# Chunk bounds from fp16 halves, q rings filled by transfers, and a new order, in a chunk-selecting attention with a feed-forward layer

## The chip, the cores and the metric

The kernel runs on one core of a Trainium2 chip. The core has five engines that run side by side, each through its own list of instructions in order: TensorE (matmuls; PE in the profile, with its weight loads as PEld), VectorE (DVE), ScalarE (ACT), GpSimd (POOL) and SyncE (SP, which here only issues transfers). The metric is the device time of one execution in microseconds, the median of the runs.

## The reference

Attention over 4 batches, 8 heads, 768 positions and head width 64, in which each query sees only six chunks of 32 keys, followed by a normalised feed-forward layer. Cut to what matters:

```python
k_min = np.min(k_chunks, axis=3)                  # per chunk of 32 keys
k_max = np.max(k_chunks, axis=3)
ub = np.sum(np.maximum(q * k_min, q * k_max), -1) # upper bound of a query with a chunk
ub = np.where(causal, ub, -1e9)
top_chunks = np.argsort(ub, axis=-1)[..., -6:]
scores = scale * q @ k.T
scores = np.where(chosen chunk and pos_q >= pos_k, scores, -1e9)
attn = softmax(scores) @ v
# x = attn with the heads side by side: (4, 768, 512)
xn = (x - mean) / sqrt(var + 1e-6) * g_ln
out = x + relu(xn @ w_ch1) @ w_ch2                # hidden width 2048
```

The bounds decide which chunks are chosen, so they need nearly fp32 accuracy: two chunks whose bounds are close must not change places.

## The kernel before

Two heads are handled together as a pair: head 0 on partitions 0 to 63, head 1 on 64 to 127. There are 16 pairs, four for each batch; pairs 0 to 3 (batch 0) take another path through loads and turning than pairs 4 to 15 (`HP` is 4). For pairs 4 to 15, q and k come in by 128-byte rows so that a VectorE transpose of 32x32 blocks turns them (`turn`); the parts that matter:

```python
prp = ctx.enter_context(tc.tile_pool(name="prp", bufs=2))
...
def turn(g, nm, i=None):
    if g >= HP:
        t = prp.tile([P, S], F32, name=nm + "T", tag=nm + "T")
        nc.vector.transpose(t, st[g][nm].rearrange("p c e -> p (c e)"))
        ...
def qpos(g, i=None):                     # relu of q; pairs 4 to 15 on VectorE
    ...
            else:
                nc.vector.tensor_scalar_max(st[g][nm][:, u:], qt[:, u:], 0.0)
                st[g]["q32"] = qt
def qring(g, i=None):                    # q as fp16 into the rings, times 128
    nc.scalar.activation(QA[g % NK][0:64, ...], qt[0:64, :], ACTF.Copy, scale=QS)
    nc.scalar.activation(QB[g % NK][64:P, ...], qt[64:P, :], ACTF.Copy, scale=QS)
def kbound(g, i=None):                   # chunk minima and maxima of k
    nc.vector.tensor_reduce(kc[:, 0, n], view, axis=AX.X, op=ALU.min)
    nc.vector.tensor_reduce(kc[:, 1, n], view, axis=AX.X, op=ALU.max)
def kdiag(g, i=None):                    # one block for each head, on GpSimd for g >= HP
    ...
        eng.tensor_tensor(kc[:, 1], kc[:, 1], kc[:, 0], ALU.subtract)
    eng.tensor_tensor(bd, kc..., hsel..., ALU.mult)
def bounds(g, i=None, idle=0):
    ...
    nc.tensor.matmul(ub, ident_b, causb[...], start=True, stop=False)   # causal -1e30
    for s in range(a, z):                # 5 query tiles
        for nm, arr in (("q32", 0), ("r32", 1)):
            nc.tensor.matmul(ub[:, s - a]..., st[g][nm][:, ...],        # fp32, 48 columns
                             st[g]["bd"][:, arr], start=False, stop=...)
def select(g, i=None):                   # threshold by the 8 greatest; then the mask
    for s in range(z - a):
        for hh in range(2):
            nc.vector.max(m8[:, s, hh, :], ub[:, s, hh, :])
    nc.vector.tensor_tensor(mn..., ub, m8[..., 6:7]..., ALU.is_le)
```

The bound is written as q times k_min plus relu(q) times (k_max minus k_min), so that two products give it. After `select`, `maskt` turns the mask on TensorE and `mring` copies it beside q into the ring; `smm` forms scores from the rings, `sexp` the exponentials on ScalarE, `diag` the causal edge on GpSimd, `values` the product with v, `norm` the division. `pstat`, `centre`, `xt`, `xcopy`, `m1`, `relu`, `m2`, `rstd` and `fin` are the feed-forward layer of each half batch. All steps stand in one string, `ORDER`, and on every engine the instructions run in its order; the engines wait for each other by data alone. `idle` and `warm` are matmuls without a use of their result[...].

Of the kernel before, what the change touches and what calls it, by code (L numbers as in the profile page):

```python
# [19 lines left out]
def kernel(  # L20
# [30 lines left out]
    QS = 128.0  # L51
    HS = 64.0
# [6 lines left out]
    vap = ctx.enter_context(tc.tile_pool(name="vap", bufs=6))  # L59
# [15 lines left out]
    causb = const.tile([P, NT - 1, 2, NCH], BF16, name="causb", tag="causb")  # L75
    RT = const.tile([P, S], F16, name="RT", tag="RT")
# [9 lines left out]
    BD = [ring.tile([P, 2, 2, NCH], F32, name=f"BD{i}", tag=f"BD{i}") for i in range(NB)]  # L86
    NM = 3
# [14 lines left out]
    def consts():  # L102
# [18 lines left out]
        nc.vector.memset(hsel[0:64, 0, 1:2], -1.0)  # L121
        nc.vector.memset(hsel[64:P, 0, 0:1], -1.0)
        nc.vector.memset(hsel[0:64, 1:3, 1:2], 1.0)
        nc.vector.memset(hsel[64:P, 1:3, 0:1], 1.0)
# [6 lines left out]
    def late():  # L131
        nc.gpsimd.memset(mhalf, -0.5)

# [67 lines left out]
    def turn(g, nm, i=None):  # L201
        if g >= HP:
            t = prp.tile([P, S], F32, name=nm + "T", tag=nm + "T")
            nc.vector.transpose(t, st[g][nm].rearrange("p c e -> p (c e)"))
            st[g][nm, i] = t
            return
        pst = ps_t.tile([P, 512], F32, name="tr", tag="one")
        src = st[g][nm, i]
        for t in range(TR):
            nc.tensor.transpose(pst[:, t * P:(t + 1) * P], src[:, t], ident_f)  # L210
        st[g][nm, i] = pst[:, 0:TR * P]

    def qpos(g, i=None):
        qt = st[g]["qn", i]
        a, z = span(g, i)
        u = P if a == 0 else 0
        signs = (("q32", -1.0), ("r32", 1.0)) if g < HP else (("r32", 1.0),)
        for nm, sign in signs:
            st[g][nm] = prp.tile([P, qt.shape[1]], F32, name=nm, tag=nm)
            if g < HP:  # L220
                nc.scalar.activation(st[g][nm][:, u:], qt[:, u:], ACTF.Relu, scale=sign)
            else:
                nc.vector.tensor_scalar_max(st[g][nm][:, u:], qt[:, u:], 0.0)
                st[g]["q32"] = qt

    def qring(g, i=None):
        qt = st[g]["qn", i]
        a, z = span(g, i)
        nc.scalar.activation(QA[g % NK][0:64, a * P:z * P], qt[0:64, :], ACTF.Copy, scale=QS)  # L229
        nc.scalar.activation(QB[g % NK][64:P, a * P:z * P], qt[64:P, :], ACTF.Copy, scale=QS)  # L230

# [20 lines left out]
    def kdiag(g, i=None):  # L252
# [10 lines left out]
        )  # L263

    def bounds(g, i=None, idle=0):
        a, z, n = chosen(g, i)
        full = ps_t.tile([P, 512], F32, name="ub", tag="one")
# [15 lines left out]
    def select(g, i=None):  # L283
# [3 lines left out]
        m8 = smp.tile([P, NT - 1, 2, 8], F32, name="m8", tag="m8")  # L287
        for s in range(z - a):
            for hh in range(2):
                nc.vector.max(m8[:, s, hh, :], ub[:, s, hh, :])  # L290
# [193 lines left out]
    def fin(b, r, i, e=None):  # L484
# [13 lines left out]
        rinit.0 ld.0.0 ld.1.0 rinit.2 rinit.3 ldv.0.0 ld.2.0 rinit.1 consts warm.8 ld.3.0 ldv.0.1 turn.0.kn.0  # L498
        turn.0.qn.0 kbound.0.0 kdiag.0.0 rrows.1.1 ld.0.1 ldv.2.0 qpos.0.0 kcopy.0.0 turn.1.kn.0 rrows.0.0 kcopy.1.0
        qring.0.0 bounds.0.0.6 turn.1.qn.0 turn.2.kn.0 qpos.1.0 kbound.1.0 select.0.0 maskt.0.0 kdiag.1.0 qring.1.0  # L500
        rrows.3.0 ldv.1.0 kbound.2.0 mring.0.0 bounds.1.0.6 turn.2.qn.0 rrows.1.0 kcopy.2.0 smm.0.0.0 qpos.2.0
        rrows.2.0 ldv.3.0 turn.3.kn.0 kdiag.2.0 select.1.0 bounds.2.0.6 maskt.1.0 kbound.3.0 mring.1.0 qring.2.0
        sexp.0.0.0 select.2.0 smm.0.0.1 kcopy.3.0 turn.3.qn.0 sexp.0.0.1 qpos.3.0 diag.0.0 smm.1.0.0 turn.0.kn.1
        maskt.2.0 qring.3.0 kdiag.3.0 sexp.1.0.0 w1.1.3 bounds.3.0.6 values.0.0 kbound.0.1 mring.2.0 smm.1.0.1
        kcopy.0.1 select.3.0 diag.1.0 smm.2.0.0 w1.0.2 norm.0.0 maskt.3.0 sexp.1.0.1 mring.3.0 values.1.0 smm.2.0.1
        norm.1.0 sexp.2.0.0 sexp.2.0.1 pstat.0.0 smm.3.0.0 diag.2.0 sexp.3.0.0 values.2.0 smm.3.0.1 pstat.1.0
        diag.3.0 sexp.3.0.1 norm.2.0 values.3.0 pstat.2.0 norm.3.0 w1.2.3 w1.3.3 pstat.3.0 ld.1.1 turn.0.qn.1
        kdiag.0.1 qpos.0.1 qring.0.1 turn.1.qn.1 centre.0.0 turn.1.kn.1 idle.5 qpos.1.1 ld.3.1 kcopy.1.1 ld.2.1
        ldv.1.1 kbound.1.1 w2.2.1 idle.4 w2.0.0 w2.1.0 qring.1.1 xt.0.0.3 ldb.4.kn xt.0.0.0 xt.0.0.2 xcopy.0.0.0
        xt.0.0.1 xcopy.0.0.2 xcopy.0.0.3 rrows.3.1 xcopy.0.0.1 bounds.0.1 ldb.4.qn rrows.0.1 turn.2.kn.1 select.0.1  # L510
        m1.0.0.0 kcopy.2.1 relu.0.0.0 turn.2.qn.1 qring.2.1 late maskt.0.1 kbound.2.1 mring.0.1 kdiag.1.1 rstd.0.0
        kdiag.2.1 m1.0.0.2 relu.0.0.2 qpos.2.1 m1.0.0.6 relu.0.0.6 m1.0.0.8 m1.0.0.4 turn.4.kn relu.0.0.8 relu.0.0.4
        m1.0.0.10 smm.0.1.0 bounds.1.1 turn.3.kn.1 relu.0.0.10 select.1.1 smm.0.1.1 sexp.0.1.0 sexp.0.1.1
        turn.3.qn.1 ldb.5.kn qpos.3.1 m1.0.0.12 kbound.4 kbound.3.1 relu.0.0.12 maskt.1.1 m1.0.0.14 smm.0.1.2
        bounds.2.1 kdiag.3.1 turn.4.qn kcopy.3.1 mring.1.1 w2.3.1 relu.0.0.14 smm.0.1.3 qpos.4 sexp.0.1.2 kdiag.4
        bounds.3.1 ldb.5.qn qring.3.1 smm.1.1.0 rrows.2.1 select.2.1 sexp.0.1.3 bounds.4 diag.0.1 sexp.1.1.0
        smm.1.1.3 sexp.1.1.3 select.3.1 smm.1.1.2 sexp.1.1.2 maskt.2.1 select.4 maskt.3.1 values.0.1 mring.2.1
        smm.1.1.1 m2.0.0.0.0 diag.1.1 kcopy.4 smm.2.1.0 m2.0.0.1.0 mring.3.1 sexp.1.1.1 smm.2.1.2 ldv.2.1 values.1.1
        sexp.2.1.0 sexp.2.1.2 norm.0.1 turn.5.kn smm.2.1.1 ldv.3.1 maskt.4 kbound.5 smm.3.1.0 pstat.0.1 m2.0.0.1.1
        sexp.2.1.1 norm.1.1 mring.4 m2.0.0.0.1 sexp.3.1.0 smm.2.1.3 turn.5.qn kdiag.5 qring.4 diag.3.1 smm.3.1.2  # L520
        sexp.2.1.3 m2.0.0.1.2 m2.0.0.0.2 sexp.3.1.2 smm.3.1.3 sexp.3.1.3 ldb.6.kn smm.4.1.0 diag.2.1 pstat.1.1
        m2.0.0.0.3 qring.5 fin.0.0.0 ldb.7.kn ldb.6.qn ldv.4 m2.0.0.1.3 smm.3.1.1 ldb.7.qn ldb.8.kn sexp.3.1.1
        ldb.8.qn ldv.6 fin.0.0.1 values.2.1 m2.0.0.2.0 sexp.4.1.0 ldv.5 values.3.1 qpos.5 smm.4.0.0 norm.2.1 kcopy.5
        m2.0.0.2.1 pstat.2.1 smm.4.1.3 sexp.4.0.0 norm.3.1 m2.0.0.2.2 diag.4.0 sexp.4.1.3 smm.4.1.1 m2.0.0.2.3
        smm.4.1.2 pstat.3.1 centre.0.1 sexp.4.1.1 sexp.4.1.2 fin.0.0.2 xt.0.1.1 smm.4.0.1 xt.0.1.3 xt.0.1.0 xt.0.1.2
        ldv.9 ldb.9.kn xcopy.0.1.0 xcopy.0.1.1 xcopy.0.1.2 bounds.5 xcopy.0.1.3 sexp.4.0.1 diag.4.1 turn.6.kn
        m1.0.1.0 kcopy.6 ldb.9.qn m1.0.1.2 relu.0.1.0 select.5 maskt.5 m1.0.1.4 relu.0.1.2 relu.0.1.4 m1.0.1.8
        turn.7.kn m1.0.1.6 relu.0.1.8 m1.0.1.14 relu.0.1.6 kbound.6 kdiag.6 ldv.7 values.4.0 mring.5 turn.6.qn
        kbound.7 qpos.6 kdiag.7 relu.0.1.14 smm.5.0.0 values.4.1 sexp.5.0.0 smm.5.0.1 rstd.0.1 bounds.6 norm.4.0
        pstat.4.0 turn.7.qn sexp.5.0.1 diag.5.0 qring.6 smm.5.1.0 values.5.0 qpos.7 smm.5.1.1 sexp.5.1.0 norm.5.0  # L530
        norm.4.1 bounds.7 sexp.5.1.1 kcopy.7 select.6 m1.0.1.10 m1.0.1.12 relu.0.1.10 maskt.6 select.7 mring.6
        smm.5.1.2 m2.0.1.0.0 relu.0.1.12 smm.5.1.3 diag.5.1 m2.0.1.0.1 sexp.5.1.2 sexp.5.1.3 maskt.7 smm.6.0.0
        turn.8.kn qring.7 kbound.8 turn.8.qn smm.6.1.0 m2.0.1.0.2 sexp.6.0.0 values.5.1 ldv.8 smm.6.0.1 kdiag.8
        m2.0.1.0.3 sexp.6.1.0 mring.7 qpos.8 smm.6.1.3 sexp.6.0.1 sexp.6.1.3 diag.6.0 smm.7.0.0 sexp.7.0.0 fin.0.1.0
        bounds.8 smm.7.1.0 pstat.5.0 smm.7.1.2 sexp.7.1.0 sexp.7.1.2 values.6.0 ldb.10.qn ldb.10.kn diag.6.1
        norm.5.1 ldb.11.qn select.8 m2.0.1.1.0 diag.7.0 norm.6.0 smm.7.0.1 sexp.7.0.1 turn.9.kn kcopy.8 maskt.8
        pstat.6.0 m2.0.1.1.1 mring.8 smm.6.1.2 sexp.6.1.2 qring.8 values.7.0 norm.7.0 smm.7.1.1 sexp.7.1.1
        m2.0.1.2.0 m2.0.1.1.2 m2.0.1.2.1 smm.6.1.1 m2.0.1.1.3 smm.7.1.3 sexp.6.1.1 kbound.9 m2.0.1.2.2 pstat.7.0
        smm.8.0.0 m2.0.1.2.3 fin.0.1.1 sexp.7.1.3 smm.8.0.1 values.6.1 sexp.8.0.0 sexp.8.0.1 centre.1.0 xt.1.0.0
        diag.7.1 ldv.10 smm.8.1.0 fin.0.1.2 xt.1.0.3 smm.8.1.3 ldb.12.kn kdiag.9 ldv.13 xcopy.1.0.0 norm.6.1  # L540
# [93 lines left out]
```

## Time and profile before

| | before |
|---|---|
| median of 3 runs | 301.5 us (301.45 to 303.76) |
| span of the profiled execution | 299.9 us |
| mean granted TensorE clock | 0.988 |
| bounds matmuls, relu half (128x48 fp32) | 144, of them 120 in pairs 4 to 15; 275 ns each as recorded |
| relu of q on VectorE (128x640 fp32) | 12, 590 ns each |
| q ring copies on ScalarE (64x768) | 24, 842 and 840 ns each |
| turns of q and of k on VectorE | 12 and 12, 966 and 964 ns each |
| transfers | 26.63 MB, 89 GB/s in the mean |

A profile row names an engine, an operation, what it writes and reads (partitions x elements and type), how often, the busy time and the mean of one. Lengths of matmuls overlap, as the next one starts while the last one drains; what one costs is read from the start of one to the start of the next. The number after L is the line of the kernel.

### The profile page before, as it was taken

The page shows a single profiled execution, that of the slowest core. Times are in us where ns is not written, and L with a number is a line of the kernel's source. Part 1 is how long each engine was busy: PE and PEld are TensorE (multiplying, and loading weights), DVE is VectorE, ACT ScalarE, POOL GpSimd, SP SyncE. Part 2 cuts the span into 40 slices and gives each one's busy share as a digit, 9 for nine tenths or more (in the row PEclk, how much of TensorE's full clock was granted, in tenths as well). Part 3 has the DMA queues.
Part 4 walks back from the last instruction along what each step waited for, and adds up shares of the span by engine and source line. Part 5 has one row for each costly group of instructions (what it writes and reads, how often), then busy time and mean ns, then how long its engine had stood idle before and what let it go on. Part 6 is the DMA issues. An engine that isn't in the chain of part 4 may idle for free.

```text
span 299.9 us, 6684 instructions
## 1 busy us (share of the span) xinstructions
PE 288.8 (96%) x2637; PEld 199.3 (66%) x2637; DVE 185.0 (62%) x595; ACT 204.6 (68%) x274; POOL 80.6 (27%) x136
## 2 busy tenths in 40 slices
PE   5897999999999999999999999999999999999994
PEld 3785678766778685867676766578766654654543
DVE  4978819767896888896887776855637601401112
ACT  2897778799868979879789779676666541522520
POOL 8737421561343252230422303002403000010000
PEclk9897999999999999999999999999999999999999
DMA  8999999709999369995297130110050100200202
GB/s 139 200 172 199 196 215 162 75 6 148 146 139 171 27 120 142 169 133 50 59 148 102 10 55 0 63 44 1 2 89 9 37 0 25 82 0 13 94 0 105
DMA packets 121469, 26.63 MB, mean 89 GB/s; under 512 B 114144, under 2 KB 118496, under 8 KB 121440
## 3 DMA queue, kind: packets, MB, share of 16 engines
q1 hardware_dynamic: 91664, 18.88, 35.0%
q0 software_dynamic: 29248, 7.34, 25.2%
q8 instruction: 20, 0.33, 0.4%
q10 hardware_dynamic: 528, 0.00, 0.1%
q14 instruction: 9, 0.07, 0.1%
HBM read 27.27 MB, written 6.29 MB: 112 GB/s over the span
## 4 chain that ended last, share of the span: by engine, by line
PE 88%; ACT 7%; DVE 1%; issue 1%; POOL 1%; DVEq 0%; ACTq 0%; POOLq 0%
PE mm L457 28%; PE yp L479 26%; PE ub L278 11%; PE mm L355 11%; PE sm L382 6%; ACT pt L363 3%; PE trh L439 2%; PE trh L300 1%; PE tr L210 1%; PE junk L311 1%; ACT KB L247 1%; ACT KA L246 1%; ACT QB L230 1%; ACT QA L229 1%; POOL pt L370 1%
## 5 line engine op out<-in xcount | busy, mean ns | idle before, releaser
L363 ACT ACTIVATE pt<-mm 128x1024 f16<-128x1024 f32 (+2 forms) x96 | 84.8, 916 | 21.3 <-PE mm L355 20.2
L479 PE MATMUL yp<-w2b,hT 128*128 128x512 f16 (+2 forms) x400 | 92.5, 370 | 0.0
L457 PE MATMUL mm<-xT,w1b 128*128 128x384 f16 x512 | 88.6, 326 | 0.0
L466 ACT ACTIVATE hT<-mm 128x768 f16<-128x768 f32 x64 | 51.7, 811 | 50.7 <-PE mm L457 50.4
L457 PEld LDWEIGHTS <-w1b 128*128 128x128 f16 x512 | 49.4, 98 | 31.6
L479 PEld LDWEIGHTS <-hT 128*128 128x128 f16 x400 | 37.6, 98 | 33.8
L488 DVE SCALAR_TENSOR_TENSOR ot<-yp,rstd,x 128x512 f32<-128x512 f32 (+2 forms) x25 | 17.9, 722 | 60.1 <-PE yp L479 42.6
L370 POOL TENSOR_SCALAR_AFFINE_SELECT pt<-pt 128x768 f16<-128x768 f16 x32 | 28.4, 898 | 67.0 <-ACT pt L363 67.0
L355 PE MATMUL mm<-QA,KA 128*128 128x128 f16 (+2 forms) x224 | 34.3, 247 | 0.6 <-ACT pt L363 0.4
L355 PE MATMUL mm<-QB,KB 128*128 128x128 f16 (+2 forms) x224 | 34.4, 247 | 0.0
L278 PE MATMUL ub<-BD,r 128*128 128x48 f32 (+1 forms) x160 | 31.1, 276 | 0.0
L382 PE MATMUL sm<-va,pt 128*128 128x65 f16 x672 | 25.6, 193 | 1.7 <-POOL pt L370 1.4
L382 PEld LDWEIGHTS <-pt 128*128 128x128 f16 x672 | 24.1, 98 | 4.8 <-POOL pt L370 2.1
L290 DVE MAX8 m<-ub 128x8 f32<-128x24 f32 (+1 forms) x160 | 16.0, 172 | 16.5 <-PE ub L278 16.4
L278 PEld LDWEIGHTS ub<-BD,r 128*128 128x128 f32 x160 | 24.5, 194 | 0.0
L355 PEld LDWEIGHTS <-KA 128*128 128x128 f16 x224 | 18.4, 101 | 9.1 <-issue 1.2
L433 POOL TENSOR_TENSOR rstd<-ve,mhalf 128x3 f32<-128x3 f32 x8 | 7.4, 923 | 58.0 <-DVE ve L430 57.9
L278 PE MATMUL ub<-BD,qnT 128*128 128x48 f32 x120 | 22.5, 269 | 0.0
L412 DVE BATCH_NORM_STATS2 bst<-x 128x6 f32<-128x128 f32 x96 | 20.9, 276 | 0.2
L259 POOL TENSOR_TENSOR kc<-kc 128x24 f32<-128x24 f32 x12 | 3.2, 264 | 66.3 <-DVE kc L241 66.3
L355 PEld LDWEIGHTS <-KB 128*128 128x128 f16 x224 | 18.1, 99 | 3.4 <-issue 0.2
L397 DVE TENSOR_TENSOR x<-sm,rden 128x384 f32<-128x384 f32 x32 | 17.8, 557 | 1.1
(78 smaller groups left out, 341.9 us busy)
## 6 DMA issues: line engine op xcount, KB each, us to landing
out_dram<-ot SPq DMA_DIRECT2D x23, 256.0 KB, 2.1
knb<-in_k_dram SPq DMA_DIRECT2D x48, 96.0 KB, 3.9
qnb<-in_q_dram SPq DMA_DIRECT2D x48, 96.0 KB, 3.8
va<-in_v_dram POOLq DMA_DIRECT2D x12, 192.0 KB, 5.0
w1b<-in_moe_w_ch_dram POOLq DMA_DIRECT2D x4, 512.0 KB, 6.8
w2b<-in_moe_w_ch_dram POOLq DMA_DIRECT2D x4, 512.0 KB, 10.0
raw<-in_k_dram SPq DMA_DIRECT2D x16, 96.0 KB, 3.6
raw<-in_q_dram SPq DMA_DIRECT2D x16, 96.0 KB, 4.1
```

The lines of the kernel that those rows point to most:

```text
L278: nc.tensor.matmul(ub[:, s - a].rearrange("p h c -> p (h c)"), st[g][nm][:, s * P - c:(s + 1) * P - c], st[g]["bd"][:, arr], start=False, ...
L290: nc.vector.max(m8[:, s, hh, :], ub[:, s, hh, :])
L355: nc.tensor.matmul(sc[:, hh, o:o + w * P], ks[:, t * P:(t + 1) * P], qs[:, s * P:(s + w) * P], start=True, stop=True,)
L363: nc.scalar.activation(st[g]["pt", r][:, 4 * i:4 * i + o].rearrange("p n h x -> p h n x"), st[g]["sc", r, i][:, :, 0:o * P].rearrange("p h ...
L370: nc.gpsimd.affine_select(out=dv, in_=dv, compare_op=ALU.is_ge, fill=0.0, base=0, pattern=[[0, 2 * TR], [1, P]], channel_multiplier=-1,)
L382: nc.tensor.matmul(pv[:, hh, s2, :], pt[:, where[t, s], hh, :], va[:, hh, t, 0:D + 1], start=(t == 0), stop=(t == s),)
L397: nc.vector.tensor_tensor(xh(b, r)[:, :, 2 * hp:2 * hp + 2, :].rearrange("p s h d -> p h s d"), pv[:, :, :, 0:D], rden.to_broadcast([P, 2, ...
L412: nc.vector.bn_stats(half(b, r)["st"][:, i, hp], xh(b, r)[:, i, 2 * hp:2 * hp + 2].rearrange("p h d -> p (h d)"),)
L457: nc.tensor.matmul(hp_[:, i, 0:TR * P], w1b[:, kt, (m + i) * P:(m + i + 1) * P], h["xT"][:, kt], start=(kt == 0), stop=(kt == KT1 - 1),)
L466: nc.scalar.activation(h["hT"][:, m:m + 2], h["hp", m][:, :, 0:TR * P], ACTF.Relu, scale=HS)
L479: nc.tensor.matmul(h["yp", i][:, cs], h["hT"][:, kt, i * P:(i + 1) * P], w2b[:, kt, cs], start=(kt == 0), stop=(kt == KT2 - 1),)
L488: nc.vector.scalar_tensor_tensor(ot[:, cs], h["yp", i][:, cs], h["rstd"][:, i:i + 1], xh(b, r)[:, i].rearrange("p h d -> p (h d)")[:, cs], ...
```

## The change

It replaces the fp32 bounds matmuls of pairs 4 to 15 by fp16 ones. q times 128 is split into a high fp16 half and the remainder as a low half, the chunk bounds (times 128 too) likewise; the bounds' two halves lie side by side as 96 columns, and four matmuls for each query tile (high q, low q, high relu, low relu) add up in PSUM. VectorE then adds the high columns, the low columns and the causal term, which was a matmul before. The high half of q is what the q ring needs, so two SBUF-to-SBUF transfers fill the ring in place of two ScalarE copies. To make room, the turned q and k share one tag with two buffers, and the v pool goes from six buffers to five. The whole order is laid out anew; the numbers of all other steps stay as they were.

```diff
+    KS = 128.0
-    vap = ctx.enter_context(tc.tile_pool(name="vap", bufs=6))
+    vap = ctx.enter_context(tc.tile_pool(name="vap", bufs=5))
+    causf = const.tile([P, NT - 1, 2, NCH], F32, name="causf", tag="causf")
+    BH = [ring.tile([P, 2, 2, 2, NCH], F16, name=f"BH{i}", tag=f"BH{i}") for i in range(NB)]
...
     def late():
+        nc.gpsimd.memset(causf, 0.0)
+        nc.gpsimd.affine_select(out=causf, ..., fill=CAUSAL, ...)
...
     def turn(g, nm, i=None):
-            t = prp.tile([P, S], F32, name=nm + "T", tag=nm + "T")
+            t = prp.tile([P, S], F32, name=nm + "T", tag="T")
...
-            else:
-                nc.vector.tensor_scalar_max(st[g][nm][:, u:], qt[:, u:], 0.0)
+    def qhi(g):
+        ...                                     # fp16 tiles of the two halves
+        nc.scalar.activation(st[g]["qh"], st[g]["qn", None], ACTF.Copy, scale=QS)
+    def qlo(g):
+        nc.vector.scalar_tensor_tensor(st[g]["ql"][:, P:], st[g]["qn", None][:, P:], QS,
+                                       st[g]["qh"][:, P:], op0=ALU.mult, op1=ALU.subtract)
+    def qrel(g):
+        nc.vector.tensor_scalar_max(rh, qh, 0.0)
+        nc.vector.scalar_tensor_tensor(rl, qh, 0.0, ql, op0=ALU.is_gt, op1=ALU.mult)
     def qring(g, i=None):
+        if i is None:
+            nc.sync.dma_start(QA[g % NK][0:64, :], st[g]["qh"][0:64, :])
+            nc.sync.dma_start(QB[g % NK][64:P, :], st[g]["qh"][64:P, :])
+            return
...                                             # kdiag
+        if g >= HP:
+            nc.gpsimd.tensor_copy(bh[:, :, 0], bd)
+            nc.gpsimd.tensor_tensor(bh[:, :, 1], bd, bh[:, :, 0], ALU.subtract)
     def bounds(g, i=None, idle=0):
+        if g >= HP:
+            ub = st[g]["ub"] = ps_t.tile([P, NT - 1, 2, 2, NCH], F32, name="ub2", tag="one")
+            for s in range(a, z):
+                for e, (nm, arr) in enumerate((("qh", 0), ("ql", 0), ("rh", 1), ("rl", 1))):
+                    nc.tensor.matmul(ub[:, s - 1]..., st[g][nm][:, s * P:(s + 1) * P],
+                                     BH[g % NB][:, arr]..., start=(e == 0), stop=(e == 3))
+            return
     def select(g, i=None):
+        if g >= HP:
+            nc.vector.tensor_tensor(ubt, ub[:, :, 1], causf, ALU.add)
+            nc.vector.tensor_tensor(ubm, ub[:, :, 0], ubt, ALU.add)
...
-        rinit.0 ld.0.0 ld.1.0 rinit.2 rinit.3 ldv.0.0 ld.2.0 rinit.1 consts warm.8 ld.3.0 ldv.0.1 turn.0.kn.0
+        ld.0.0 ld.1.0 ld.2.0 ldv.2.0 ld.3.0 ld.1.1 ld.0.1 ldv.1.0 consts rinit.1 warm.8 rinit.2 turn.0.kn.0
...                                             # the rest of the order, new throughout
```

## The prediction

> **What bounds the kernel now.** I read first the busy shares and the 40 slices of the page:
>
> ```profile
> span 299.9 us, 6684 instructions
> PE 288.8 (96%) x2637; PEld 199.3 (66%) x2637; DVE 185.0 (62%) x595; ACT 204.6 (68%) x274; POOL 80.6 (27%) x136
> PE   5897999999999999999999999999999999999994
> ...
> DVE  4978819767896888896887776855637601401112
> PEclk9897999999999999999999999999999999999999
> ```
>
> TensorE works from slice 4 to the end without a gap at full granted clock. VectorE is at seven to nine tenths up to about 180 us, and nearly free from 240 us. A busy share can flatter, so next the chain of waits of the page (shares of the span by engine, then by line):
>
> ```profile
> PE 88%; ACT 7%; DVE 1%; issue 1%; POOL 1%; DVEq 0%; ACTq 0%; POOLq 0%
> PE mm L457 28%; PE yp L479 26%; PE ub L278 11%; PE mm L355 11%; PE sm L382 6%; ACT pt L363 3%; PE trh L439 2%; PE trh L300 1%; PE tr L210 1%; PE junk L311 1%; ACT KB L247 1%; ACT KA L246 1%; ACT QB L230 1%; ACT QA L229 1%; POOL pt L370 1%
> ```
>
> TensorE carries 88% of the chain; the rest lies in the first 60 us. In the list of waits (engine, line, releaser: us in total, times, longest) its first entry is the start, and all of its entries together are under 7 us; VectorE waits for TensorE instead:
>
> ```profile
> PE junk L311 <- DVE MN L126: 3.1, 1, 3.1
> ...
> DVE m L290 <- PE ub L278: 16.4, 9, 6.0
> ```
>  So a microsecond of TensorE work taken out is nearly a microsecond of time, as long as the others keep up. The bounds (ub) are 11% of the chain. One head pair's bounds, from the timeline around 105 us (start, length, engine, count last):
>
> ```profile
> 105.19 0.39 PE L355 MATMUL mm<-QA,KA 128*128 128x128 f16 x4
> 105.41 0.39 PE L355 MATMUL mm<-QB,KB 128*128 128x128 f16 x4
> 105.63 0.27 PE L274 MATMUL ub<-causb,ident_b 128*128 128x240 bf16 x1
> 105.74 0.33 PE L278 MATMUL ub<-BD,qnT 128*128 128x48 f32 x2
> 105.90 0.39 PE L278 MATMUL ub<-BD,r 128*128 128x48 f32 x2
> ...
> 107.69 0.39 PE L278 MATMUL ub<-BD,r 128*128 128x48 f32 x2
> 107.91 0.39 PE L355 MATMUL mm<-QA,KA 128*128 128x128 f16 x4
> ...
> 119.35 1.07 PE L382 MATMUL sm<-va,pt 128*128 128x65 f16 x30
> 120.26 0.33 PE L439 MATMUL trh<-ident_h,xc 128*128 128x128 f16 x3
> ```
>
> Here starts matter, not lengths, because matmuls overlap. The bounds hold TensorE from 105.63 to 107.91: 2.28 us, of which each fp32 matmul of only 48 columns takes 0.111 (two in 0.22). Four fp16 matmuls of 128 columns take 0.22, 0.056 each; thirty of 65 columns take 0.91, 0.030 each.
>
> Last, the stages: busy time in 30 us stretches (length, then PE, PEld, DVE, ACT, POOL).
>
> ```profile
> 90.00:120.00 30.00, 30.00 (x312) 22.19 (x312) 24.11 (x77) 25.82 (x31) 9.88 (x16) 1.00 0.87 115
> 120.00:150.00 30.00, 30.00 (x318) 22.15 (x315) 24.88 (x75) 25.17 (x32) 8.45 (x11) 1.00 0.70 103
> 240.00:270.00 30.00, 30.00 (x175) 16.32 (x174) 5.03 (x13) 9.49 (x14) 0.85 (x1) 1.00 0.07 27
> ```
>
> VectorE is 80 to 83% busy in the middle, so it has room for 5 us in 30, and no more. That is the number on which the case turns.
>
> **What the Trainium skill says.** "TensorE: Matmul & The Clock Gate", section "Wait — 56ns, not 53.3ns?", gives the pace of warm back-to-back matmuls as columns over 2.4 GHz and about 2.5 ns. The 0.056 for 128 columns agrees; for 96 columns it gives 42.5 ns. "FP8 and Floating Point Precision", section "TensorE Precision Notes", has a true fp32 product as four passes (high and low halves against each other); 48 columns four times are 80 ns, and the trace shows 111, so the fp32 form also pays something beyond its passes. "VectorE: DVE Perf Modes", section "The perf-mode tier table", caps two-tensor operations at one element per cycle in fp32 or from PSUM, and lets a one-tensor fp16 operation in SBUF run at four. The trace agrees for the first: 384 elements (norm) against 240 (the comparison) differ by 0.16 us from start to start, 1.1 ns per element. "DMA: Bandwidth & Descriptors", section "Anatomy of one DMA", gives a fixed cost of about 2 us for each transfer; the small loads here land 3.7 to 4.1 us after issue, because the engines are shared.
>
> **The change part by part**, each for one head pair of batches 1 to 3 (12 of them).
>
> *TensorE.* Out: 20 fp32 matmuls and the causal one, 2.28 us. In: 20 fp16 matmuls of 96 columns (high and low half of the chunk bounds side by side). Between 65 columns at 30.3 and 128 at 55.8 ns the line gives 42.8 ns, together 0.86. Saved: 1.42, times 12 = 17.1 us. All of it lies in the stage that TensorE fills.
>
> *ScalarE.* Out: the two fp16 copies into the q rings, 0.84 each. In: one copy of the whole turned tile to fp16, same length of 768, so 0.84. It gains 0.84 x 12 = 10 us. It isn't the bound; the waits for the exponentials in the first 60 us don't touch these operations.
>
> *VectorE.* Out: the relu of q, 0.59 by its row (128x640 f32, mean 590 ns). In, estimated from rows of before: the low half (two tensors, 640 elements, fp32 in): 0.32 for 240 elements start to start and 400 more at 1.1 ns, 0.75; the relu of the high half, fp16 and one tensor: 0.3, by the 64x384 fp16 copy at 0.26; the low half gated by the sign: two tensors, 0.75, or about 0.4 if it runs at two; two additions over 240 elements (low plus causal, then high) at 0.32 to 0.41: 0.7. Together 2.1 to 2.5 in and 0.59 out. I take 1.85 more, near the upper end, times 12 = 22 us: VectorE goes from 185 to about 207.
>
> *GpSimd.* Two more operations of 96 elements, at the 0.37 of the BD product: 0.75 x 12 = 9 us, on an engine at 27%. They lengthen the way from the reductions to the bounds by 0.75 us; the new order has to hide it.
>
> *Transfers.* Two of 96 KB per pair fill the q rings, on the same issuing queue as the loads. In before, four load issues take that queue 2.5 to 5 us while the engines are full. Counted in the new order, at least 45 steps lie between the later of what a ring transfer waits for (the copy to fp16, the entry before it on its queue) and the first score matmul that reads the ring. I count 4 to 8 us for issue and landing; hidden as a rule.
>
> *Buffers and order.* The turned q and k tiles now share two buffers where they had two each, so the next turn waits until ScalarE has copied the last but one. The first twelve steps put more loads and two v loads ahead of the constants: identity and causal mask, made on GpSimd, come later by the 1.7 us of one v load's issue, while the memset that TensorE's first wait is for comes earlier by about 1 us. I set the start at zero, give or take 1.5.
>
> **The sum by stage.** I added such durations along the old and the new order (matmuls start to start) up to three marks, in us:
>
> - selection of pair 11: TensorE 137 before, 126 after; VectorE 122 before, 133 after
> - last norm of pair 15: TensorE 217, then 203; VectorE 175, then 193
> - whole: TensorE 277, then 259; VectorE 187, then 209
>
> In before, the bounds of pair 11 end at 155.3 us and its selection at 156.7, that is 19.5 over TensorE's sum (start, idle and warming matmuls, slow first clock). By TensorE alone the changed kernel would be there at 126 + 19.5 = 145. VectorE would then have to be busy 133 of 145, 92%, against 122 of 156.7, 78%, in before. Its best 20 us stretch in before was 17.5, 87%. At 90% it gets there at 148, at 87% at 153. What follows the mark is 143.2 us in before, less 5.6 of saved matmuls: 137.6, with VectorE at half load. Span: 145 + 137.6 = 283 without loss, 286 at 90%, 291 at 87%. Time is 1.6 over the span (301.5 and 299.9): 284 to 292. I take 289: 17 saved, about 4.5 given back to VectorE.
>
> **Rivals.**
> - *TensorE's saving arrives whole: 284.* For it: VectorE's idle time in before is mostly waiting for TensorE (16.4 us for the bounds, and more for the layer's results), which a new order can use; ScalarE gets lighter. Against: 92% on an in-order engine for 145 us.
> - *VectorE becomes the bound in the middle: 293 to 298.* For it: the sums above, and that its one-tensor fp32 operations take 0.4 us in some places and 1.1 in others, so the added ones may do so too. Against: from 180 us it is free, and the layer's matmuls can be set between.
> - *The ring transfers or shared turn buffers put new waits in front of the score matmuls: 295 to 303.* For it: loads fill the transfer engines to nine tenths until 100 us, and one queue serves all. Against: the distance in the order, and 1.5 KB rows instead of the loads' 128-byte ones.
> - *The start grows by late constants: plus 2 on any of these.*
>
> **Range and chances.** The saving is certain in size, the giving back isn't: 284 to 296 in 8 of 10. Faster by over 2% means under 295.5: all but the worst of the second rival and the third, 0.85; within 2% 0.12; slower 0.03.
>
> **What would show it.** The ub matmuls: 240 of fp16 with 96 columns, 0.86 us per pair from start to start. VectorE's busy time 205 to 211. TensorE's busy time about 272, and its idle time 13 to 17 us instead of 11, the new part before 155 us and released by VectorE (masks, turned tiles or x). The selection of pair 11 ends near 149. Wrong would be: fp16 matmuls slower than 50 ns each, waits of TensorE on the ring transfers, or a VectorE that loses nothing.

## The result, and the profile after

The changed kernel takes 289.83 us (median of 4 runs) against 302.29: a ratio of 0.957, with a 95% interval of 0.952 to 0.963. The page of the changed kernel (busy shares, then slices):

```profile
span 288.4 us, 6771 instructions
PE 273.3 (95%) x2625; PEld 181.3 (63%) x2625; DVE 207.8 (72%) x643; ACT 191.2 (66%) x262; POOL 90.3 (31%) x162
PE   6785999999999999999999999999999999999994
...
DVE  4698678999999899989899979797847735001111
```

TensorE is still full from slice 5 on, and VectorE is now at nine tenths in most slices from 40 to 160 us. The chain of waits has moved only in part; bounds (ub) are 4% of it, no longer 11%:

```profile
PE 71%; ACT 10%; DMA 6%; DVE 4%; SPq 4%; issue 2%; POOL 2%; DVEq 0%; ACTq 0%; POOLq 0%
```

The same two stretches of both kernels follow (length, then busy time of PE, PEld, DVE, ACT, POOL, then granted clock, transfers). Before:

```profile
0.00:40.00 40.00, 33.27 (x275) 25.07 (x276) 30.46 (x120) 28.70 (x57) 25.38 (x49) 0.91 1.28 183
40.00:140.00 100.00, 99.66 (x1057) 74.61 (x1054) 77.72 (x238) 84.17 (x104) 32.38 (x52) 1.00 0.97 122
```

After:

```profile
0.00:40.00 40.00, 30.80 (x258) 22.57 (x259) 28.76 (x116) 26.46 (x55) 26.65 (x52) 0.96 1.29 173
40.00:140.00 100.00, 98.08 (x1074) 68.57 (x1073) 92.99 (x272) 84.29 (x108) 34.60 (x63) 1.00 0.96 130
```

TensorE stands 9.2 us in the first 40 instead of 6.7, and 1.9 instead of 0.3 in the next 100. VectorE goes from 78 to 93% there. ScalarE, relieved of ring copies, is as busy as before in 100 us, because more of the other work now falls into them.

One pair's bounds in the changed kernel, from the timeline of TensorE:

```profile
56.10 0.25 PE L297 MATMUL ub<-BH,q 128*128 128x96 f16 x2
56.19 0.25 PE L297 MATMUL ub<-BH,r 128*128 128x96 f16 x2
...
56.87 0.25 PE L297 MATMUL ub<-BH,r 128*128 128x96 f16 x2
56.95 0.33 PE L396 MATMUL mm<-QA,KA 128*128 128x384 f16 x1
```

From 56.10 to 56.95 are 0.85 us, where 2.28 stood. Twelve times 1.43 is 17.2 us of TensorE, and the span fell by 11.5. So 5.7 were given back. Who took them, the list of waits begins to show: TensorE's longest in the changed kernel (us in total, times, longest).

```profile
PE mm L396 <- ACT pt L404: 2.7, 5, 1.0
PE tr L218 <- ACT r L226: 1.9, 2, 1.0
PE junk L352 <- DVE MN L129: 1.8, 1, 1.8
PE sm L423 <- POOL pt L411: 1.2, 1, 1.2
```

Five waits end with an exponential on ScalarE (pt). VectorE ends only one of these, the first memset. From 40 us on the list is short: three waits for pt (0.8 us), two for a layer output of ScalarE (hT, 0.7), one for a mask from VectorE (0.3); before has one wait there, 0.2 us for pt.

A finer measure, used below: from each matmul's start to the next I took off what the first should hold the array (columns over 2.4 GHz plus 2.5 ns, the form named in the prediction, which the 65-, 96- and 128-column rows fit; 112 ns for fp32 ones) and added up what is left over where it is more than 60 ns, with the time before the first matmul. Up to 40 us this **lag** is 12.8 us before and 15.8 after; from 40 us on it is 0.8 and 3.7. The start thus gives back 3.0 and the rest 2.9, together 5.9, where the spans say 5.7. Part of the 3.0 is the clock of this one execution: another execution of the changed kernel, at a mean clock of 0.999, has a span of 286.8 us, while before at 0.999 has 299.8. That is 13.0 less, so 4.2 given back; if the 2.9 hold there too, some 1.3 are left for the start.

### The profile page after: what moved, and what is told of

Read it like the earlier page. It is cut to its first block, busy times and chain, and to the rows that moved or that the text cites. A ratio compares the mean times of both kernels' runs of the same rounds, so it can differ in the third digit from the quotient of the medians.

```text
span 288.4 us, 6771 instructions
## 1 busy us (share of the span) xinstructions
PE 273.3 (95%) x2625; PEld 181.3 (63%) x2625; DVE 207.8 (72%) x643; ACT 191.2 (66%) x262; POOL 90.3 (31%) x162
## 4 chain that ended last, share of the span: by engine, by line
PE 71%; ACT 10%; DMA 6%; DVE 4%; SPq 4%; issue 2%; POOL 2%; DVEq 0%; ACTq 0%; POOLq 0%
PE yp L520 27%; PE mm L498 21%; PE mm L396 10%; DMA knb<-in_k_dram 6%; PE sm L423 6%; SPq L177 4%; ACT pt L404 3%; PE ub L297 3%; ACT KB L269 2%; PE trh L480 1%; ACT KA L268 1%; PE ub L313 1%; PE trh L341 1%; POOL va L196 1%; ACT hT L507 1%
## 5 line engine op out<-in xcount | busy, mean ns | idle before, releaser
L491 DVE TENSOR_SCALAR xT<-trh,gstr 128x384 f16<-128x384 f16 x16 | 6.4, 413 | 18.1 <-PE trh L480 18.1
L281 POOL TENSOR_TENSOR kc<-kc 128x24 f32<-128x24 f32 x12 | 3.9, 328 | 34.3 <-DVE kc L263 34.2
L489 ACT ACTIVATE xT<-trh,gstr 128x384 f16<-128x384 f16 x16 | 8.9, 581 | 7.3 <-PE trh L480 7.1
L346 DVE COPY QA<-trh 64x640 f16<-64x640 f16 (+2 forms) x20 | 8.6, 428 | 7.0 <-PE trh L341 6.6
L189 POOL DMA_DIRECT2D va<-in_v_dram x12 | 12.8, 1062 | 0.0
```

The source lines that it names most:

```text
L189: nc.gpsimd.dma_start(va[:, :, :, 0:D].rearrange("p h t d -> p (h t) d"), v[b, 2 * hp:2 * hp + 2].rearrange("h (t p) d -> p (h t) d", p=P),)
```

## The experiments

All twelve in one table. "Pairs 5 to 15" is the time from the first bounds matmul of pair 5 to that of pair 15; "lag" is the measure above, after 40 us. A low clock in the first 40 us makes a span longer by itself (the section on the start has the numbers), so the stretch says more than the span.

| run | ratio to before (95%) | span | first layer matmul | first bounds of pair 4 | pairs 5 to 15 | lag |
|---|---|---|---|---|---|---|
| before | 1 | 299.9 | 34.3 | | | 0.8 |
| changed | 0.957 (0.952 to 0.963) | 288.4 | 37.7 | 56.1 | 145.9 | 3.7 |
| e1_old_start | 0.957 (0.951 to 0.962) | 287.2 | 35.0 | 54.7 | 145.9 | 4.5 |
| e2_less_dve | 0.959 (0.952 to 0.967) | 289.9 | 39.1 | 57.5 | 145.9 | 3.8 |
| e3_less_pe | 0.949 (0.943 to 0.955) | 284.8 | 37.1 | 55.6 | 143.2 | 5.6 |
| e4_old_order | 1.051 (1.046 to 1.056) | 315.7 | 34.2 | | | 31.9 |
| e5_start | 0.965 (0.958 to 0.972) | 291.7 | 34.6 | 59.3 | 145.9 | 9.5 |
| e6_less_act | 0.957 (0.952 to 0.962) | 288.2 | 36.0 | 53.8 | 145.4 | 4.9 |
| e7_ring_act | 1.001 (0.996 to 1.006) | 300.1 | 36.0 | 57.8 | 156.2 | 16.5 |
| e8_old_ops | 1.036 (1.027 to 1.044) | 314.1 | 40.7 | 60.5 | 164.7 | 9.2 |
| f1_w2_late | 0.962 (0.958 to 0.966) | 288.9 | 37.0 | 55.5 | 145.9 | 4.7 |
| f2_start_w2 | 0.956 (0.952 to 0.959) | 287.5 | 35.3 | 54.0 | 145.9 | 4.7 |
| f3_start_w2_act | 0.960 (0.957 to 0.964) | 288.6 | 35.0 | 54.2 | 147.3 | 6.1 |
| f4_more_dve | 0.971 (0.967 to 0.976) | 291.7 | 37.1 | 55.5 | 149.3 | 7.3 |

My theory was V, as predicted: VectorE gives the time back in the middle. The rivals were S (the start gives it back) and C (ScalarE does), and later D (the early transfers do).

**e2_less_dve: less VectorE work.**

```diff
     def qrel(g):
         nc.vector.tensor_scalar_max(rh, qh, 0.0)
-        nc.vector.scalar_tensor_tensor(rl, qh, 0.0, ql, op0=ALU.is_gt, op1=ALU.mult)
     def bounds(g, i=None, idle=0):
-                for e, (nm, arr) in enumerate((("qh", 0), ("ql", 0), ("rh", 1), ("rl", 1))):
+                for e, (nm, arr) in enumerate((("qh", 0), ("ql", 0), ("rh", 1), ("ql", 1))):
```

> The changed kernel without the VectorE product that gates the low half of q by its sign: 12 instructions of 0.82 us, 9.8 us of VectorE work left out; the fourth matmul reads the ungated low half instead, so TensorE does the same work (bounds lose their last bits). Theory V: 3 to 4 us faster, about 286. Theory S: VectorE isn't what ends the waits, at most 1.3 us faster, 288.5 to 290.

The stretch from pair 5 to 15 is 145.9 us, as in the changed kernel, with 8.0 us less VectorE work over the kernel (199.8 against 207.8). The longer span comes from the first 40 us, where the clock was granted at 0.82 and 0.84. V has fallen for the changed kernel: VectorE's load isn't what TensorE waits for there.

**f4_more_dve: more of it.** The same line is there twice.

```diff
         nc.vector.scalar_tensor_tensor(rl, qh, 0.0, ql, op0=ALU.is_gt, op1=ALU.mult)
+        nc.vector.scalar_tensor_tensor(rl, qh, 0.0, ql, op0=ALU.is_gt, op1=ALU.mult)
```

> The changed kernel with the gating product on VectorE done twice: 12 instructions of 0.82 us, 9.8 us more VectorE work, at 95% busy. Leaving 9.8 us out had changed nothing. If VectorE still has room, 290 to 291; if the changed kernel stands just at the edge of it, most of the 8 instructions that lie before pair 12 are paid: 294 to 297.

The time rose to 293.92 us and the stretch by 3.4, just short of the second expectation. The waits now include one for VectorE that the changed kernel doesn't have (PE ub, r being the gated half of q):

```profile
PE mm L397 <- ACT pt L405: 3.6, 7, 1.6
...
PE ub L298 <- DVE r L243: 0.9, 2, 0.6
```

So the changed kernel stands at the edge: 8 us less are worth nothing, 9.2 us more cost about 4. VectorE's reserve was greater than the prediction took it to be. Whether the 4 us are due to the load or to the place of the doubled product, right in front of the bounds that read it, isn't separated.

**e3_less_pe: less TensorE work.**

```diff
-                for e, (nm, arr) in enumerate((("qh", 0), ("ql", 0), ("rh", 1), ("rl", 1))):
+                for e, (nm, arr) in enumerate((("qh", 0), ("rh", 1))):
```

> The changed kernel without the two matmuls of each query tile that take the low half of q: 120 matmuls at 0.043 us, 5.1 us of TensorE work left out, VectorE work the same (bounds lose their last bits). If TensorE sets the pace throughout, all 5.1 come off: about 284.7. If VectorE sets it up to pair 11 (theory V), only the third that lies behind it counts: 1.7 off, about 288.

The low halves of q are left out of the bounds, 5.1 us of matmuls. The span fell by 3.6 us and the median to 286.8, between the two expectations. The lag after 40 us rose from 3.7 to 5.6, by 1.9 of the 5.1. TensorE sets the pace, but with so little reserve behind it that two fifths of a further gain are lost.

**e7_ring_act: the transfers undone.**

```diff
     def qring(g, i=None):
         if i is None:
-            nc.sync.dma_start(QA[g % NK][0:64, :], st[g]["qh"][0:64, :])
-            nc.sync.dma_start(QB[g % NK][64:P, :], st[g]["qh"][64:P, :])
+            nc.scalar.copy(QA[g % NK][0:64, :], st[g]["qh"][0:64, :])
+            nc.scalar.copy(QB[g % NK][64:P, :], st[g]["qh"][64:P, :])
```

> One part of the change undone: the q rings are filled by two ScalarE copies of the fp16 tile (64x768) instead of two transfers; 24 copies of about 0.83 us put 20 us back on ScalarE, at the same places of the order. Theory C: they stand in front of exponentials and layer outputs, and a third to a half of them is paid: 296 to 300. Rival (ScalarE at 66% has room): 289 to 291.

This takes away the whole gain: a ratio of 1.001, 0.996 to 1.006. TensorE does the cheap bounds here too, and VectorE the same work; only ScalarE carries 19.4 us more (210.6 against 191.2). TensorE's waits:

```profile
PE mm L396 <- ACT pt L404: 7.8, 9, 1.4
PE mm L498 <- ACT hT L507: 4.1, 3, 2.2
PE junk L352 <- DVE MN L129: 1.8, 1, 1.8
PE mm L396 <- ACT hT L507: 1.4, 2, 1.2
```

These lines have 13.3 us of waits that end with ScalarE, where the changed kernel has 3.4; from 40 us on it is 11.6 against 1.5. One of them in the timeline (all engines; the bracket is the idle time before and its releaser):

```profile
105.84 0.82 ACT L246 COPY QA<-q 64x768 f16<-64x768 f16 x1
...
106.67 0.83 ACT L247 COPY QB<-q 64x768 f16<-64x768 f16 x1
106.68 0.39 PE L396 MATMUL mm<-QA,KA 128*128 128x128 f16 x4
...
107.53 2.64 ACT L404 ACTIVATE pt<-mm 128x1024 f16<-128x1024 f32 x3
...
108.60 0.32 PE L396 MATMUL mm<-QA,KA 128*128 128x384 f16 x1 [1.31 <-ACT pt L404]
```

The two ring copies hold ScalarE from 105.84 to 107.5; the exponential behind them frees the score buffer only at 108.6, and the score matmuls stand for it 1.3 us. There are two such buffers (`ps_m`), and here they didn't bridge 1.7 us of other ScalarE work. The amount of work alone doesn't decide it: before has as many ring copies in its own order, ScalarE 204.6 us busy, and TensorE waits 0.2 us for it after 40. So e7 shows what the transfers are worth in this order; an order laid out for the copies might lose less, and that wasn't tried.

**e6_less_act: still less ScalarE work.**

```diff
     def kcopy(g, i=None):
-        nc.scalar.copy(KB[g % NK][64:P, a * P:z * P], kt[64:P, :])
+        if g < HP:
+            nc.scalar.copy(KB[g % NK][64:P, a * P:z * P], kt[64:P, :])
```

> The changed kernel without the second of the two ScalarE copies that fill the k ring, in pairs 4 to 15: 12 copies of 0.83 us, 10 us of ScalarE work left out (head 1 of these pairs scores against old keys). Theory C (after 40 us TensorE is held 3.7 us in all, mostly where a score or layer matmul waits for a buffer that ScalarE empties, and ScalarE is busy with copies then): the 3.7 falls to about 1.5 and the time by 2, to 287.5. Rival (these waits come from the order of dependencies and not from ScalarE's load): at most 0.5 faster, 289 to 290.

Head 1 of pairs 4 to 15 scores against old keys here. The time didn't change (0.957), as the rival said; the stretch is 0.5 shorter. So the transfers' 20 us are worth 12, these 10 next to nothing; as they stand in other places of the order, amount and place aren't separated by this pair of runs.

**e8_old_ops and e4_old_order: operations and order apart.** The first has the operations of before in the new order, the second the reverse:

```diff
# e8, over before:    ORDER of the changed kernel, qpos.g where qlo.g stands; no qhi, qrel
# e4, over changed:   ORDER of before, qhi.g qlo.g qrel.g where qpos.g stood
-            t = prp.tile([P, S], F32, name=nm + "T", tag="T")
+            t = prp.tile([P, S], F32, name=nm + "T", tag="T", bufs=3)
-    ldp = ctx.enter_context(tc.tile_pool(name="ldp", bufs=7))
+    ldp = ctx.enter_context(tc.tile_pool(name="ldp", bufs=6))
```

> The operations of before in the new order: the fp32 bounds, the relu of q where the low half of q was formed, the ring copies on ScalarE where the transfers stood. If the gain is TensorE's 17.2 us of cheaper bounds alone, this is 290 plus 17, and the 20 us of ScalarE copies may add to it: 305 to 310. Rival (a good part of the gain is the new order, and it serves the old operations too): 297 to 300.

> The operations of the changed kernel in the order of before: the three new q steps stand where the relu stood (four times a step earlier, where the ring fill came before it), three shared turn buffers instead of two and six load buffers instead of seven, as that order needs. Theory V: the old order has no room for VectorE's added work where it puts it, 293 to 298. Theory S: the old start is 3 us better and the order hardly matters otherwise, 286 to 290.

314.41 and 317.75 us: each half alone, put together in this way, is slower than before. The old operations gain nothing from the new order; they lose 12 us by it, 4.4 more than the top of the first expectation. After 40 us TensorE's waits in e8 come to 7.2 us, and all end with ScalarE, which is no fuller than in before (203.8 and 204.6 us). That points to the places of its copies and not to their amount. Another part is the start, whose first 25 us ran at half pace in this execution (0.107 us for a matmul of 128 columns, 0.055 after that). The new operations in the old order lag by 31.9 us after 40: the three q steps stand right before what needs them. In its lists of waits (engine, line, releaser):

```profile
DVE q L235 <- ACT q L232: 9.5, 8, 2.5
...
ACT q L232 <- DVE qnT L212: 12.7, 4, 8.7
...
PE mm L498 <- ACT hT L507: 7.5, 2, 7.3
```

At the longest place ScalarE waits 8.7 us for a turned q, behind it in its queue stands a layer output, and TensorE waits 7.3 us for that. VectorE, which turns that q at 174.01, doesn't wait meanwhile: it is busy 13.93 of the 14.25 us from 160.75 on, with work that stands in front of the turn. Another 4.6 us of TensorE's waits are for the low (1.7) and the gated half of q (2.9) from VectorE. So theory V, which fell for the new order, names what happens in the old one, with far too small a loss (293 to 298). (e4 has one load buffer less and a third turn buffer; what these do wasn't tried apart.) Neither theory saw that the order is a condition of the gain rather than a share of it.

**e1, e5, f1, f2: the start.** The old start is the order of before up to the first layer matmul. e5 takes it for TensorE, VectorE and ScalarE alone, up to the centring, with the transfers where the changed kernel has them and the constants ahead of the v loads. f1 issues the w2 loads late, f2 does both.

```diff
# f1, f2
-    ... kdiag.2.1 m1.0.0.2 w2.1.0 ... w2.0.0 ... w2.2.1 ... w2.3.1 ... kdiag.4 ...
+    ... kdiag.2.1 m1.0.0.2 ... kdiag.4 w2.0.4 w2.1.4 w2.2.4 w2.3.4 ...
```

> The changed kernel with the order of before up to the first feed-forward matmul, and its own order after that. In the changed kernel that matmul starts at 37.7 us, in before at 34.5. Theory S (the start gives back about 3 us, the rest of the order runs as dense as before): the matmul starts near 34.5 and the time falls by 2.5 to 3.5, to about 287. Theory V (VectorE, 95% busy from 60 to 160 us, gives back the 4 to 5 us in the middle): the earlier start is eaten by VectorE later on, and the time stays within 1 us, 289 to 290.

> The changed kernel with a start in which TensorE, VectorE and ScalarE follow the order of before up to the centring of the first half batch, while loads and weights keep the changed kernel's positions, and the constants stand ahead of the v loads on GpSimd. In the first 40 us TensorE's starts are 14.0 us behind the pace of its matmuls in the changed kernel, 9.8 in before. Theory S: that gap falls to 10 or 11, nothing is given back after it because the loads aren't late as they were with the whole old start, and the time is 286 to 287. Rival (what the start gains is eaten before pair 4 anyhow): 288.5 to 289.5.

> The changed kernel with the four loads of w2 (512 KB each) issued after pair 4's bounds block on GpSimd, about 46 us, instead of from 33.8 us; nothing else moves. Theory D (the transfer engines are full until 55 us, and the k load of pair 5, issued by 40 us, lands behind the w2 loads at 52.5 us; VectorE, which takes its work in order, stands or runs late there): that load lands 5 us or more earlier, the 2 us by which TensorE is held between 50 and 61 us fall to 1, and the time by about 1: 288.5 to 289.5. If the w2 loads come too late for their first use (62 us), 2 us or more slower.

> The changed kernel with both: the start of run e5_start and the late w2 loads. Theory D: the start's 3 us were lost again only because pair 4's and pair 5's loads lay behind the weights (VectorE stood 6.5 us for one); now they stay: 286 to 287. Rival (the first 60 us are bound by something else as well, ScalarE's copies say): 289 or more.

(The 14.0 and 9.8 us in e5's expectation are the lag up to 40 us without the time before the first matmul.) In e1 the first layer matmul comes 2.7 us earlier, at pair 4 1.4 are left, and the span is 1.2 shorter; the median moved by 0.3. In e5 it comes 3.1 us earlier, and pair 4 comes 3.2 later. VectorE's timeline in e5 says why:

```profile
48.59 0.98 DVE L212 STREAM_TRANSPOSE knT<-knb 128x768 f32<-128x768 f32 x1 [6.54 <-DMA knb<-in_k_dram]
```

It stood 6.5 us for pair 4's k, which landed behind weights; TensorE waited 3.7 for a mask behind it. With the w2 loads late (f2) that wait is gone and pair 4 comes at 54.0, 2.1 earlier than in the changed kernel, so theory D holds for e5. But 1.1 of the 2.1 are lost before pair 5 (it comes at 63.8, in the changed kernel at 64.8). TensorE's timeline in f2 shows two places:

```profile
57.45 0.99 PE L423 MATMUL sm<-va,pt 128*128 128x65 f16 x27 [0.53 <-POOL pt L411]
...
59.97 0.45 PE L341 MATMUL trh<-ident_h,MN 128*128 128x128 f16 x5 [0.75 <-DVE MN L332]
```

The first is of my making: the four w2 issues hold GpSimd from 50.0 to 55.0 us, and the causal edge of the exponentials stands behind them. The second is a mask from VectorE, for which TensorE waits 0.75 us, in the changed kernel 0.30. The median of f2 is 289.23, no clear gain. In f1 the k of pair 5 is turned at 51.6 instead of 52.6 us, 0.65 of that is how much earlier that run was at pair 4, and the time isn't better.

Much in these comparisons is the clock of single executions and not the order. e6 and e7 have the start of the changed kernel as it is. With a granted clock of 1.00 from 20 to 40 us their first layer matmul comes at 36.0; the changed kernel's own trace has 0.91 there and 37.7, e2 0.84 and 39.1. The nine idle matmuls in front of it show it, in the changed kernel and then in e7:

```profile
32.20 3.35 PE L357 MATMUL idle<-MN 128*128 128x512 f16 x9
31.79 2.11 PE L357 MATMUL idle<-MN 128*128 128x512 f16 x9
```

At a clock of 1.00 the old start (e4, 34.2) is thus ahead by 1.8 us and not by 3.4, and e6 is at pair 4 at 53.8 with the start unchanged (one k copy less before it), as early as f2. Nor does f1, at 0.90, refute D: in e6 VectorE stands 2.3 us for pair 5's k (0.3 in the changed kernel's trace), TensorE 2.9 us for a mask behind it, and pair 5 comes at 65.0, no earlier than in the slower start. There the load takes back what the clock had gained.

**f3: ScalarE's order.** Over f2, five copies moved behind evacuations: `kcopy.4` after `relu.0.0.6`, `qring.3.1` after `relu.0.0.12`, `kcopy.8` after `relu.0.1.8`, `qhi.8` after `sexp.5.1.0`, `qhi.11` after `sexp.9.1.1`.

> As f2_start_w2, and five ScalarE copies moved behind the evacuations they stood in front of (k copies of pairs 4 and 8, the q copies of pairs 8 and 11 and of one batch-0 pair). Theory C in its second form (not ScalarE's load but its order at four places holds TensorE, 0.4 to 0.6 us each): 1 to 1.5 faster than f2_start_w2, about 285.5. Rival (each wait moves to the next place, as when 10 us of copies were left out): within 0.5 of it.

The median is 1.4 us slower than f2's instead of faster: of the waits for score buffers one went (0.4 us at 137.6), the pair near 95 us grew from 0.8 to 1.4, and one for a mask came (0.7 at 144.6). Moving single copies by hand doesn't beat this order; none of the versions that do all the work is clearly faster than the changed kernel.

## Why the prediction was right

- **TensorE's term was right**: 0.86 us per pair predicted and 0.85 measured, 17.1 and 17.2 in the sum. The busy time came to 273 (272 predicted), the idle time to 15.1 us (13 to 17). GpSimd's two operations took 8.1 us (9 predicted).
- **VectorE's added work was right in the sum**: 22 predicted, 207.8 less 185.0, 22.7 measured. Its parts were not all: the gating product took 0.82 in fp16, as long as the fp32 one (0.81), and not the 0.4 that the prediction held possible; the fp16 relu took 0.45 in the mean instead of 0.3.
- **What was given back was right in size and wrong in place.** The step "4.5 given back to VectorE" between 145 and 149 us failed. 5.7 were given back between the two traces: 3.0 in the start, which the prediction "set at zero" (about half of that is the clock), and 2.9 after 40 us, in waits that mostly end with ScalarE; taking 8 us from VectorE (e2) brought nothing. What would recover those 2.9 isn't settled: leaving out 10 us of ScalarE copies (e6) brought nothing either, and moving five of them (f3) cost 1.4. Yet even the mark seemed to confirm the step: pair 11's selection ended at 151.7 us (149 predicted), VectorE busy 133.2 of them (133 predicted), 88%. That was luck, the sum of the start's delay and the small waits.
- **VectorE's limit was set too low.** The 90% that the prediction took for it isn't one: VectorE runs at 93% for 100 us here, and at 97% in f4, where TensorE loses 3.6 us more. Nor was 87% its best in before: the prediction's 17.5 of 20 us are 18.1 from 117 to 137 us.
- **ScalarE's term was wrong in kind.** The gain of 10 us came to 13.4, but "It isn't the bound" treated the transfers as a help without weight. e7 shows that in this order nothing of TensorE's 17.2 us arrives without them. The reason that the prediction still came out is that the change brings both parts together.
- **The ring transfers are hidden**, as predicted: they land 2.9 and 2.8 us after issue (4 to 8 with issue predicted), and TensorE has no wait for them (in the old order, e4, one of 2.3 us). That the engines are at nine tenths until 100 us was not so throughout: from 60 to 67.5 us before has 0.09.
- **The order** was taken as something that might cost 2 us in the start. The start cost 3.0 in this trace; but e4 and e8, each slower than before, show that operations and order gain only together.

How the start loses its 3 us, and why a better one (e1, f2) keeps only about 1 of them, is settled only in part: some 1.6 of the 3.4 us at the first layer matmul are the clock, the old start recovers the rest, loads, GpSimd's queue or a mask take most of that again, and a start that is better for all wasn't found.

## What to carry to other kernels

When the fullest engine gets lighter by 17 us, ask of each neighbour what it can deliver in the shorter time, by its worst place and not by its mean: in e7 a ScalarE at 70% cost the whole gain, because its copies stood in front of two score buffers, while before, at 68% with as many copies in other places, lost next to nothing. The order is part of such a change; the parts should be tried with the order they were made for, and each part undone alone, before any of them is called small. And a right total can hide two wrong terms: the time alone wouldn't have told. Before two starts are compared, compare the clock that each execution was granted.

## What the runs showed of the hardware that was not expected

- A two-tensor VectorE operation with a constant (scalar_tensor_tensor) over 640 elements took 0.82 us with fp16 in and out (806 to 851 ns) and 0.81 with fp32 in: no gain from the shorter type.
- An SBUF-to-SBUF transfer of 96 KB in rows of 1.5 KB landed 2.0 to 5.6 us after issue, 2.9 in the middle, while the loads from DRAM by 128-byte rows took 3.8 in the same run.
- ScalarE took 0.83 us to copy 64x768 from fp16 to fp16, as long as the casts from fp32 (0.83) and as the whole 128x768 tile (0.84): half the partitions cost the same, so one copy of the whole tile takes ScalarE half of what two half copies take.
